# Linear attention with a token mixer: from head pairs to units of 256 tokens, all engines on a planned order

## The chip, the core and the metric

One core of a Trainium2 chip runs the kernel. Its engines are TensorE (PE, with its weight loads shown apart as PEld), VectorE (DVE), ScalarE (ACT), GpSimd (POOL) and SyncE (SP), which here only issues transfers; 16 DMA engines move the data. Each engine takes its instructions strictly in the order in which they were put into its queue, and waits on semaphores for the others. The metric is the device time of one execution in microseconds, the median over the runs.

## The reference, cut to what matters

```python
B, H, S, D = 4, 8, 768, 48
for t in range(S):                                  # float32, per batch and head
    cur   = (u * k[t])[:, None] * v[t][None, :]
    y[t]  = r[t] @ (state + cur)
    state = w[t][:, None] * state + k[t][:, None] * v[t][None, :]
x = y laid out as [B, S, 384]
W = (x @ w_q) @ (x @ w_k).T / 8                     # 64 hidden columns
out = relu(W @ x) @ w_out                           # [B, S, 384] float32
```

Both kernels work in chunks of 128 tokens. With L the running sum of log w inside a chunk, r is scaled by exp(L before t), k by exp(-L at t); the product of the two, masked to earlier tokens, times v gives the part of y that comes from inside the chunk. A state per head pair carries the rest, and u enters as a term on the diagonal. The mixer has no softmax, so W @ x is taken as (x w_q) (T), with T = (x w_k).T @ x summed over all 768 tokens of a batch: the second half of the mixer can start only when a batch's last token has its y.

## The kernel before, in words

For each batch, `prep` runs for four pairs of heads, each over all 768 tokens (6 chunks). It loads w, k, r, v (L127), takes the logarithm (L144), sums it twice on PE (cw), takes two exponentials (L151, L158), multiplies them with r on DVE (`RdS`, L166) and with k on POOL (`KdS`, L168), transposes both on PE (psT) and copies the result out of PSUM (`RKT`, L177). The masked products are `AmB` (L188). POOL also builds the u term in three more passes (L195, L196, L199) with a reduction on DVE between them (L198). Then a loop over the six chunks of the batch carries the state (`SB`, L238), forms `X` (L250) and transposes it (`XT`, L260). After it come the mixer's products, `mixT` (L288), the last product `fps`, its copy `osb` (L296), and one store for each chunk (L297).

The order in each queue is the framework's own: it lets prep of one batch run beside the chunk loop of the one before. All loads and stores go through the SP queue: each load waits for a free one of three buffers of its kind, each store for its osb, and what stands behind waits too. All matmuls go through the helper at L54, so rows of PE are told apart by their tiles.

Of the kernel before, what the change touches and what calls it, by code (L numbers as in the profile page):

```python
# [25 lines left out]
def kernel(  # L26
# [43 lines left out]
    iota1 = consts.tile([C, 1], mybir.dt.int32, tag="iota1")  # L70
    nc.gpsimd.iota(iota1, pattern=[[0, 1]], base=1, channel_multiplier=1)
    bias_px = consts.tile([C, 1], F32, tag="bpx")
    bias_mi = consts.tile([C, 1], F32, tag="bmi")
    bias_c = consts.tile([C, 1], F32, tag="bc")
    nc.scalar.activation(bias_px, iota0, ACT.Copy, bias=0.0, scale=MU)
    nc.scalar.activation(bias_mi, iota1, ACT.Copy, bias=0.0, scale=-MU)
    nc.gpsimd.memset(bias_c, MU * C)

    NB = 3
    LW = []
    RdS = []
    for i in range(NB):
        t = consts.tile([C, NCH, C], BF16, name=f"logw{i}", tag=f"logw{i}")
        nc.gpsimd.memset(t, 0.0)
        LW.append(t)
        t = consts.tile([C, NCH, C], BF16, name=f"RdS{i}", tag=f"RdS{i}")
        nc.gpsimd.memset(t, 0.0)
        RdS.append(t)  # L90
    KdS = []
    PT = []
    for i in range(2):
        t = consts.tile([C, NP, NCH, C], BF16, name=f"KdS{i}", tag=f"KdS{i}")
# [16 lines left out]
    sm = ctx.enter_context(tc.tile_pool(name="sm", bufs=3))
    ps = ctx.enter_context(tc.tile_pool(name="ps", bufs=1, space=bass.MemoryType.PSUM))
    xpool = ctx.enter_context(tc.tile_pool(name="xpool", bufs=2))
    msb = ctx.enter_context(tc.tile_pool(name="msb", bufs=2))
    mout = ctx.enter_context(tc.tile_pool(name="mout", bufs=4))

    def mtile(shape, dtype, name):
        return ps.tile(shape, dtype, name=name, tag="m", bufs=2)

    def prep(b, hp, AmB, RKT, VB, Vd, ptp):  # L120
        n = b * NP + hp
        wG = ld.tile([C, 2 * NCH, D], F32, name="wG", tag="wG")
        kG = ld.tile([C, 2 * NCH, D], F32, name="kG", tag="kG")
        rG = ld.tile([C, 2 * NCH, D], F32, name="rG", tag="rG")
        vG = ld.tile([C, 2 * NCH, D], F32, name="vG", tag="vG")
        for ap, tl in ((w, wG), (k, kG), (r, rG), (v, vG)):
            nc.sync.dma_start(out=tl, in_=ap[b, ds(hp * 2, 2)].rearrange(  # L127
                "h (c p) d -> p (h c) d", p=C))
        if n == 0:
            nc.sync.dma_start(out=u1, in_=u.rearrange("h d -> (h d)"))  # L130
            nc.gpsimd.partition_broadcast(ubc, u1)

        def hcd(t):
            return t.rearrange("p (h c) d -> p h c d", h=2)

        def chd(t):
            return t.rearrange("p (h c) d -> p c h d", h=2)

        def pad(t):
            return t.rearrange("p c (h x) -> p c h x", h=2)[:, :, :, 0:D]  # L140

        logw = LW[n % NB]
        for hh in range(2):
            nc.scalar.activation(logw[:, :, ds(hh * 64, D)],  # L144
                                 wG[:, ds(hh * NCH, NCH)], ACT.Ln,
                                 bias=0.0, scale=LN_SCALE)
        cw1 = ps.tile([C, 2, 512], F32, name="cw1", tag="cw")
        for hh in range(2):
            mm(cw1[:, hh, 0:NCH * D], US128, logw[:, :, ds(hh * 64, D)])
        ecwx = hw.tile([C, 2, NCH, D], BF16, name="ecwx", tag="ecwx")  # L150
        nc.scalar.activation(ecwx.rearrange("p h c d -> p h (c d)"),  # L151
                             cw1[:, :, 0:NCH * D], ACT.Exp,
                             bias=bias_px, scale=1.0)
        cw0 = ps.tile([C, 2, 512], F32, name="cw0", tag="cw")
        for hh in range(2):
            mm(cw0[:, hh, 0:NCH * D], U128, logw[:, :, ds(hh * 64, D)])
        emcw = hw.tile([C, 2, NCH, D], BF16, name="emcw", tag="emcw")
        nc.scalar.activation(emcw.rearrange("p h c d -> p h (c d)"),  # L158
                             cw0[:, :, 0:NCH * D], ACT.Exp,
                             bias=bias_mi, scale=-1.0)  # L160
        for c in range(NCH):
            mm(ptp[:, hp, ds(c, 1)], logw[:, c], ones)

        Rd = RdS[n % NB]
        Kd = KdS[b % 2][:, hp]
        nc.vector.tensor_tensor(pad(Rd), chd(rG),  # L166
                                ecwx.rearrange("p h c d -> p c h d"), ALU.mult)
        nc.gpsimd.tensor_tensor(pad(Kd), chd(kG),  # L168
                                emcw.rearrange("p h c d -> p c h d"), ALU.mult)
        nc.scalar.copy(VB[:, :, ds(hp * 2, 2)], chd(vG))  # L170

        psT = ps.tile([C, 2, 1024], BF16, name="psT", tag="psT")
        for c in range(NCH):
            mm(psT[:, 0, ds(c * C, C)], Rd[:, c], ID128, trans=True)
        for c in range(NCH):
            mm(psT[:, 1, ds(c * C, C)], Kd[:, c], ID128, trans=True)
        nc.vector.tensor_copy(RKT[:, hp], psT[:, :, 0:NCH * C])  # L177

        NG = NCH // 2
        for g in range(2):  # L180
            A = ps.tile([C, 2, 512], F32, name="A", tag="A")
            for cc in range(NG):
                c = g * NG + cc
                for hh in range(2):
                    mm(A[:, hh, ds(cc * C, C)],
                       RKT[ds(hh * 64, D), hp, 1, ds(c * C, C)],
                       RKT[ds(hh * 64, D), hp, 0, ds(c * C, C)])
            nc.vector.tensor_tensor(  # L188
                AmB[:, ds(hp * 2, 2), ds(g * NG, NG)],
                A[:, :, 0:NG * C].rearrange("p h (c t) -> p h c t", c=NG),  # L190
                _rep(_rep(US128, 1, NG), 1, 2), ALU.mult)

        uk = hw.tile([C, 2, NCH, D], F32, name="uk", tag="uk")
        ubs = ubc[:, ds(hp * D2, D2)].rearrange("p (h d) -> p h d", h=2)
        nc.gpsimd.tensor_tensor(uk, hcd(kG), _rep(ubs, 2, NCH), ALU.mult)  # L195
        nc.gpsimd.tensor_tensor(uk, uk, hcd(rG), ALU.mult)  # L196
        diag = hw.tile([C, 2, NCH], F32, name="diag", tag="diag")
        nc.vector.tensor_reduce(diag, uk, axis=AX.X, op=ALU.add)  # L198
        nc.gpsimd.tensor_tensor(Vd[:, :, ds(hp * 2, 2)], VB[:, :, ds(hp * 2, 2)],  # L199
                                _rep(diag.rearrange("p h c -> p c h"), 3, D),  # L200
                                ALU.mult)
# [126 lines left out]
```

## Time and profile before

| | |
|---|---|
| Median of 3 runs (lowest, highest) | 182.39 us (180.18, 184.01) |
| Profiled execution, its span from first to last instruction | 182.1 us |
| Busy: PE, DVE, POOL, ACT | 121.0, 112.7, 95.3, 74.0 us |
| Moved by DMA, mean rate | 24.23 MB, 133 GB/s |
| Mean granted TensorE clock | 0.869 of full speed |

The page gives no other time for the profiled execution than its span; the span lies inside the range of the three runs. No engine is busy for more than two thirds of it, so the page alone names no engine as the limit: what to look for is which wait ends last in each stretch. A matmul's duration on the page is that of one instruction in a pipeline; the time that a row of matmuls takes is read from the starts of successive groups.

### The profile page before, as it was taken

What the parts mean: (1) busy time and instruction counts of PE and PEld (TensorE: products, weight loads), DVE (VectorE), ACT (ScalarE), POOL (GpSimd) and SP (SyncE); (2) the same over time, 40 slices, a digit from 0 to 9 for tenths busy, and PEclk for the clock granted to TensorE, in tenths of its full rate; (3) what the DMA queues carried; (4) which work ended last, traced back from release to release, by engine and by line L of the source; (5) the groups of instructions that cost most, each with busy time, mean ns of one, the idle gap of its engine ahead of it and who ended that gap; (6) DMA issues with size and microseconds to landing.
All of it is one profiled execution on the core that took longest, in us unless ns stands there. A gap on an engine that the chain in (4) does not pass through costs nothing.

```text
span 182.1 us, 3121 instructions
## 1 busy us (share of the span) xinstructions
PE 121.0 (66%) x1200; PEld 74.3 (41%) x1200; DVE 112.7 (62%) x156; ACT 74.0 (41%) x140; POOL 95.3 (52%) x86
## 2 busy tenths in 40 slices
PE   0152178130698787966988986688888964787791
PEld 0121045010465653343765533465564243565240
DVE  6011147469889977644799778179996553744042
ACT  3175473310045446066346461944456232022620
POOL 8410599999728976406993954379586202000000
PEclk9999999999999997585599999657999697557969
DMA  7999999999999300399999908999940240000024
GB/s 127 186 188 187 187 185 158 196 215 157 169 187 168 67 4 2 142 236 200 190 178 191 166 13 237 235 168 200 185 73 0 86 150 27 0 5 0 0 81 178
DMA packets 104000, 24.23 MB, mean 133 GB/s; under 512 B 100529, under 2 KB 103986, under 8 KB 103986
## 3 DMA queue, kind: packets, MB, share of 16 engines
q1 hardware_dynamic: 103186, 23.70, 76.7%
q0 software_dynamic: 800, 0.34, 1.5%
q8 instruction: 9, 0.15, 0.4%
q14 instruction: 5, 0.04, 0.1%
HBM read 19.66 MB, written 4.72 MB: 134 GB/s over the span
## 4 chain that ended last, share of the span: by engine, by line
PE 25%; DVE 23%; issue 18%; POOL 12%; ACT 7%; DMA 7%; SPq 6%; POOLq 1%; ACTq 0%; DVEq 0%
DVE RdS L166 6%; PE psT L54 6%; DVE X L250 5%; SPq L127 5%; DVE RKT L177 5%; POOL uk L196 4%; DMA wG<-in_w_dram 3%; ACT XT L260 3%; POOL uk L195 3%; PE cw L54 3%; POOL Vd L199 3%; PE wq_ps L54 2%; PE fps L54 2%; DVE AmB L188 2%; PE Tps L54 2%
## 5 line engine op out<-in xcount | busy, mean ns | idle before, releaser
L168 POOL TENSOR_TENSOR KdS<-kG,emcw 128x576 bf16<-128x576 f32 x16 | 22.2, 1388 | 41.5 <-ACT emcw L158 33.2
L188 DVE TENSOR_TENSOR AmB<-A,US 128x768 bf16<-128x768 f32 x32 | 30.4, 950 | 5.7 <-PE A L54 4.4
L166 DVE TENSOR_TENSOR RdS<-rG,ecwx 128x576 bf16<-128x576 f32 x16 | 20.8, 1298 | 20.2 <-ACT ecwx L151 14.6
L177 DVE COPY RKT<-psT 128x1536 bf16<-128x1536 bf16 x16 | 15.3, 953 | 19.4 <-PE psT L54 19.3
L195 POOL TENSOR_TENSOR uk<-kG,ubc 128x576 f32<-128x576 f32 x16 | 24.0, 1499 | 0.0
L196 POOL TENSOR_TENSOR uk<-uk,rG 128x576 f32<-128x576 f32 x16 | 23.6, 1476 | 0.6
L199 POOL TENSOR_TENSOR Vd<-VB,diag 128x576 bf16<-128x576 bf16 x16 | 18.7, 1172 | 8.4 <-ACT VB L170 6.2
L54 PE MATMUL A<-RKT 48*128 48x128 bf16 x192 | 17.5, 263 | 7.0 <-DVE RKT L177 4.2
L144 ACT ACTIVATE logw<-wG 128x288 bf16<-128x288 f32 x32 | 12.4, 435 | 23.7 <-PE ptp L54 11.3
L151 ACT ACTIVATE ecwx<-cw,bias_px 128x576 bf16<-128x576 f32 x16 | 11.9, 741 | 24.6 <-PE cw L54 24.5
L54 PEld LDWEIGHTS <-KdS 128*128 128x128 bf16 x176 | 16.1, 123 | 13.7 <-POOL KdS L168 9.9
L54 PEld LDWEIGHTS <-RKT 48*128 48x128 bf16 (+1 forms) x272 | 13.6, 108 | 19.6 <-issue 9.3
L54 PE MATMUL fps<-wout_sb,mixT 128*128 128x384 bf16 x72 | 19.7, 418 | 1.7 <-ACT mixT L288 1.2
L296 DVE COPY osb<-fps 128x384 f32<-128x384 f32 x24 | 13.0, 554 | 12.4 <-PE fps L54 12.2
L54 PE MATMUL cw<-logw,US 128*128 128x288 bf16 x32 | 10.5, 365 | 13.4 <-ACT logw L144 12.9
L260 ACT COPY XT<-xt_ps 128x768 bf16<-128x768 bf16 x12 | 9.6, 799 | 21.4 <-PE xt_ps L54 21.4
L158 ACT ACTIVATE emcw<-cw,bias_mi 128x576 bf16<-128x576 f32 x16 | 11.9, 742 | 11.3 <-PE cw L54 11.2
L54 PE MATMUL psT<-ID,RdS 128*128 128x128 bf16 x96 | 11.4, 272 | 7.5 <-DVE RdS L166 7.5
L54 PE MATMUL cw<-logw,U 128*128 128x288 bf16 x32 | 9.7, 386 | 8.4 <-ACT ecwx L151 8.4
L54 PE MATMUL psT<-ID,KdS 128*128 128x128 bf16 x96 | 12.7, 277 | 2.8 <-POOL KdS L168 2.8
L170 ACT CAST VB<-vG 128x576 bf16<-128x576 f32 x16 | 10.7, 666 | 7.8 <-DMA vG<-in_v_dram 7.7
L54 PE MATMUL Sn<-VB,KdS 128*128 128x96 bf16 x80 | 9.9, 238 | 5.4 <-POOL KdS L168 5.4
(53 smaller groups left out, 181.1 us busy)
## 6 DMA issues: line engine op xcount, KB each, us to landing
wG<-in_w_dram SPq DMA_DIRECT2D x16, 288.0 KB, 5.6
kG<-in_k_dram SPq DMA_DIRECT2D x16, 288.0 KB, 5.3
rG<-in_r_dram SPq DMA_DIRECT2D x16, 288.0 KB, 5.6
vG<-in_v_dram SPq DMA_DIRECT2D x16, 288.0 KB, 5.6
out_dram<-osb SPq DMA_DIRECT2D x24, 192.0 KB, 1.9
wout_sb<-in_moe_w_out_dram POOLq DMA_DIRECT2D x1, 288.0 KB, 4.8
wq_f<-in_moe_w_q_dram SPq DMA_DIRECT2D x1, 96.0 KB, 4.6
wk_sb<-in_moe_w_k_dram POOLq DMA_DIRECT2D x1, 48.0 KB, 4.6
```

Source lines behind the costliest of these rows:

```text
L54: nc.tensor.matmul(o, l, rr, start=start, stop=stop, skip_group_check=sgc, is_transpose=trans)
L144: nc.scalar.activation(logw[:, :, ds(hh * 64, D)], wG[:, ds(hh * NCH, NCH)], ACT.Ln, bias=0.0, scale=LN_SCALE)
L151: nc.scalar.activation(ecwx.rearrange("p h c d -> p h (c d)"), cw1[:, :, 0:NCH * D], ACT.Exp, bias=bias_px, scale=1.0)
L166: nc.vector.tensor_tensor(pad(Rd), chd(rG), ecwx.rearrange("p h c d -> p c h d"), ALU.mult)
L168: nc.gpsimd.tensor_tensor(pad(Kd), chd(kG), emcw.rearrange("p h c d -> p c h d"), ALU.mult)
L177: nc.vector.tensor_copy(RKT[:, hp], psT[:, :, 0:NCH * C])
L188: nc.vector.tensor_tensor(AmB[:, ds(hp * 2, 2), ds(g * NG, NG)], A[:, :, 0:NG * C].rearrange("p h (c t) -> p h c t", c=NG), _rep(_rep(US12 ...
L195: nc.gpsimd.tensor_tensor(uk, hcd(kG), _rep(ubs, 2, NCH), ALU.mult)
L196: nc.gpsimd.tensor_tensor(uk, uk, hcd(rG), ALU.mult)
L199: nc.gpsimd.tensor_tensor(Vd[:, :, ds(hp * 2, 2)], VB[:, :, ds(hp * 2, 2)], _rep(diag.rearrange("p h c -> p c h"), 3, D), ALU.mult)
L260: nc.scalar.copy(XT[:, :, ds((c - 1) * C, 2 * C)], tp)
L296: nc.vector.tensor_copy(osb, fps)
```

## The change

The whole body is new. The unit of work is 256 tokens of one batch over all eight heads (12 units, three for a batch). A load brings one tensor of a unit as 1,024 rows of 384 bytes (two tokens of a head beside each other) instead of 1,536 rows of 192 bytes, into four buffers of its kind; for seven of the twelve units v is loaded in token order instead, by four transfers over 64 partitions each with rows of 192 bytes, 2,048 rows in all; for the other five a PE product with a permutation (vp) sorts it.

The logarithm's sum is formed once and transposed (cw: channels on partitions, tokens on columns, both exponentials from it). r and k are cast to bf16 (c16, mostly on POOL) and transposed raw (rT, kT), the transposed k is copied out (ks), and the exponentials are multiplied in afterwards (RT, KT). The u term is a product on PE (qT, dps, dd) and one POOL pass (Vd). kb and kd turn the scaled k back for the state. The loop of sn, sb, y, x, xt, the mixer's qk, T, mx, rl, fp and the stores follow for each unit, with 256-token tiles. PSUM is one tile of eight banks, PS, from which steps take one or two banks.

Every step is put into a list with an engine, a planned duration and a rank. `Plan.order` gives each engine its steps by rank, walks through them with the planned durations to choose banks and a common order, and the instructions are emitted in that order with the framework's own ordering switched off. ENG gives the engine of each step for the 12 units (A, D, P for ACT, DVE, POOL). PE gets 9 filler products at the start, 26 after the first cw and 16 near the end.

```diff
+def view(t, off, dims, p0=0, pn=128):
+
+    base = t[ds(p0, pn), ds(off, 1)]
+    return dataclasses.replace(base, ap=[list(base.ap[0])] + [list(d) for d in dims])
...
+    def add(self, eng, dur, rank, fn, after=(), fill=None, read=(), lag=100, mode=0,
+            behind=None):
+        s = dict(mode=mode, behind=behind, eng=eng, dur=dur, rank=rank, fn=fn, after=[a for a in after if a is not None],
...
+    def dma(self, issue, dur, rank, fn, after=(), fill=None, read=()):
+
+        i = self.add("SP", issue, rank, fn, after, fill, read, lag=0)
+        m = self.add("DQ", dur, 0, self.nothing, [i], lag=0)
+        return i, self.add(f"L{m['n']}", 1950, 0, self.nothing, [m], lag=0)
...
+        for s in sorted(self.steps, key=lambda s: s["rank"]):
+            if s["eng"] in queues:
+                queues[s["eng"]].append(s)
...
+            if s["eng"] == "SP" and len(moved) >= 3:
+                t = max(t, moved[-3])
...
+            if s["fill"] in ("w", "s"):
+                two = s["fill"] == "w"
+                at = [clear(x) for x in owners]
+                end = 7 if two else 8
...
+            change = e == "PE" and s["mode"] != mode
+            if e == "PE":
+                mode = s["mode"]
+            run(s, t, s["dur"] + self.switch * change)
...
+    PS = ps.tile([C, 4096], F32, name="PS", tag="PS")
+    NB = 4
+    WG = [const([C, HW], F32, f"wg{i}") for i in range(NB)]
...
+    KDS = [const([C, 1024], BF16, f"kd{i}") for i in range(2)]
+    LW = [const([C, 2 * H * 64], BF16, f"lw{i}") for i in range(2)]
...
+    def load_v(b, i, tl):
+
+        for c in range(2):
+            src = v[b, :, ds(i * U + c * C, C)].rearrange("h (q j) d -> j q h d", j=2)
+            for j in range(2):
+                nc.sync.dma_start(out=view(tl, c * DM, [[D, H], [1, D]], p0=64 * j, pn=64),
+                                  in_=src[j])
+
+    def load(b, i, tl, ap):
+        nc.sync.dma_start(
+            out=view(tl, 0, [[D2, H], [1, D2]]),
+            in_=ap[b, :, ds(i * U, U)].rearrange("h (p j) d -> p h (j d)", j=2))
...
+    for _ in range(9):
+        mm(PS[:, ds(0, 512)], Z[:, ds(0, C)], Z)
...
+    ENG = dict(k16="DAPPAPPPPPPP", r16="DPPPPAPPPPPP", KT="DDPDPPPPPPPP", vb="AAAADAAAAAAA",
+               kd="AAADAAAAADAA", xts="ADDADAADAAAD", qks="AAADAAAAAAAA", rl="AAAAAAAAAAAA",
+               os="AAAAAAADDDDD", dd="AAAAAADDAAAD", ks="DDAAADADDAAD")
+    RANK = [14, 0, 0, 0, 0, 15, 0, 0, 0, 1, 0, 0, 2, 0, 0, 5, 0, 0, 0, 0, 1, 1, 3, 1, 5, 2, 5, 10,
...
+    DIRECT = "001011011011"
+    SPLIT = (0, B * NU - 1)
...
+    plan = Plan(kinds, 90)
...
+        for tile_, ap, name in ((wg, w, "wg"), (kg, k, "kg"), (rg, r, "rg"), (vg, v, "vg")):
+            if name == "vg" and direct:
+                issue, land = plan.dma(2600, 2080, STEP * n + OFF["load"],
+                                       lambda tile_=tile_: load_v(b, i, tile_), fill=name)
+            else:
+                issue, land = plan.dma(580, 1440 + 340 * (name == "wg" and n == 0),
+                                       STEP * n + OFF["load"],
...
+            nc.scalar.activation(view(lw, 0, [[64, H], [512, 2], [1, D]]),
+                                 view(wg, 0, [[D2, H], [D, 2], [1, D]]), ACT.Ln,
+                                 bias=0.0, scale=math.exp(-MU))
...
+                op = dict(A=nc.scalar.copy, D=nc.vector.tensor_copy, P=nc.gpsimd.tensor_copy)[e]
+                op(view(dst, 0, [[64, H], [512, 2], [1, D]]),
+                   view(src, 0, [[D2, H], [D, 2], [1, D]]))
...
+            t["cw"] = cw = wtile("cw")
+            for hp in range(NP):
+                for j in range(2):
+                    for c in range(2):
+                        mm(cw[:, ds(c * 512 + hp * C, C)],
+                           lw[ds(c * 64, 64), ds(j * 512 + hp * 128, 128)],
...
+                nc.scalar.activation(sb("en", [C, 1024])[:, cols(cs, 512)],
+                                     t["cw"][:, cols(cs, 512)], ACT.Exp, bias=0.0, scale=-1.0)
...
+                nc.scalar.activation(
+                    view(ep, cs[0] * NP * EW + 66, [[EW, NP * len(cs)], [-65, 2], [1, 64]]),
...
+                t[name] = x = stile(BF16, name)
+                for hp in range(NP):
+                    for j in range(2):
+                        mm(view(x, hp * C + j * 64, [[512, 2], [1, 64]]),
+                           src[:, ds(j * 512 + hp * 128, 128)], ID16, trans=True)
...
+            copy(kse, sb("ks", [C, 1024]), t["kT"])
...
+            nc.vector.tensor_tensor(sb("qT", [C, 1024]), t["rT"], t["ks"], ALU.mult)
...
+                nc.vector.tensor_tensor(
+                    view(sb("RT", [C, 1024]), cs[0] * 512, [[C, n4], [64, 2], [1, 64]]),
+                    view(t["rT"], cs[0] * 512, [[C, n4], [64, 2], [1, 64]]),
...
+                e = nc.vector if kte == "D" else nc.gpsimd
+                e.tensor_tensor(sb("KT", [C, 1024])[:, cols(cs, 512)], t["ks"][:, cols(cs, 512)],
+                                t["en"][:, cols(cs, 512)], ALU.mult)
...
+                nc.gpsimd.tensor_copy(sb("VB", [C, 2 * DM]), vg)
...
+                nc.gpsimd.tensor_copy(view(sb("v16", [C, 2 * DM]), 0, [[D, H], [DM, 2], [1, D]]),
+                                      view(vg, 0, [[D2, H], [D, 2], [1, D]]))
...
+                        mm(x[:, ds(c * 512, DM)], PM[ds(c * 64, 64), ds(j * C, C)],
+                           t["v16"][ds(c * 64, 64), ds(j * DM, DM)], start=(j == 0), stop=(j == 1))
...
+                copy(vbe, view(sb("VB", [C, 2 * DM]), 0, [[DM, 2], [1, DM]]),
+                     view(t["vp"], 0, [[512, 2], [1, DM]]))
...
+                    mm(x[:, ds(c * H + hp * 2, 2)], t["qT"][:, ds((c * NP + hp) * C, C)],
+                       UB[:, ds(hp * 2, 2)], start=(c == 0 and hp == 0), stop=True)
...
+                nc.gpsimd.tensor_tensor(
+                    sb("Vd", [C, 2 * DM])[:, cols(cs, DM)], t["VB"][:, cols(cs, DM)],
...
+                        mm(x[:, ds(hh * 512 + hp * C, C)],
+                           t["KT"][ds(hh * 64, D), ds((c * NP + hp) * C, C)],
+                           t["RT"][ds(hh * 64, D), ds((c * NP + hp) * C, C)])
...
+                nc.vector.tensor_tensor(
+                    view(sb(f"AM{c}", [C, 1024]), 0, [[C, 8], [1, C]]),
+                    view(t[f"A{c}"], 0, [[C, 8], [1, C]]),
...
+                    mm(t["kb"][:, ds(cp * C, C)], t["KT"][:, ds(cp * C, C)], ID16, trans=True)
...
+                copy(kde, view(KDS[n % 2], cs[0] * 512, of), view(t["kb"], cs[0] * 512, of), gv)
...
+                    if old is not None:
+                        mm(x[:, ds(0, DM)], ID16, old.tile, start=True, stop=False)
+                    for hp in range(NP):
+                        mm(x[:, ds(hp * D2, D2)], KDS[n % 2][:, ds((c * NP + hp) * C, C)],
+                           t["VB"][:, ds(c * DM + hp * D2, D2)],
...
+                    nc.vector.tensor_tensor(view(x, 0, [[D, H], [1, D]]),
+                                            view(t[f"sn{c}"], 0, [[D, H], [1, D]]),
+                                            view(t["ptm"], c * 8, [[1, 8], [0, D]]), ALU.mult)
...
+                    mm(y[:, ds(c * 512 + h * D, D)],
+                       t[f"AM{c}"][:, ds(hh * 512 + hp * C, C)],
+                       t["VB"][:, ds(c * DM + h * D, D)], start=(h == 0), stop=(old is None))
+                if old is not None:
+                    for hp in range(NP):
+                        mm(y[:, ds(c * 512 + hp * D2, D2)], t["RT"][:, ds((c * NP + hp) * C, C)],
...
+                nc.vector.scalar_tensor_tensor(
+                    view(X["t"], (2 * i + c0) * DM, [[DM, ncs], [1, DM]]),
+                    view(t["y"], c0 * 512, [[512, ncs], [1, DM]]), gx,
+                    view(t["Vd"], c0 * DM, [[DM, ncs], [1, DM]]), ALU.mult, ALU.add)
...
+                    mm(x[:, ds(wqo, nq)], wq_sb[:, ds(kt * C, C)], XT[:, ds(kt * nq, nq)],
+                       start=(end and kt == 0), stop=(kt == NK - 1))
...
+                    mm(x[:, ds(dt * U, U)], batch["TS"][:, ds(dt * 128, 128)],
+                       view(batch["QK"], ii * 384 + C, [[64, 2], [C, 2], [1, 64]]),
+                       start=(dt != 1))
...
+                    relu(e, view(t[f"MX{ii}"], cs[0] * C, [[U, NK], [1, w_]]),
+                         view(t[f"mx{ii}"], cs[0] * C, [[U, NK], [1, w_]]))
...
+                            mm(x[:, ds(c * 512, DM)],
+                               t[f"MX{ii}"][:, ds(kt * U + c * C, C)],
+                               wo_sb[:, ds(kt * DM, DM)], start=(kt == 0), stop=(kt == NK - 1))
...
+                if end and ii == NU - 1 and p == 0:
+                    add("A", 550, "st", f_st(nc.scalar), more=6 * ii, cs=cs, use=[go], lag=2000)
+                else:
+                    issue, land = plan.dma(
+                        500, 580 * len(cs), STEP * n + OFF["st"] + 6 * ii, f_st(nc.sync),
+                        [go.by[c] for c in cs])
...
+    for n in range(B * NU):
...
+        if n == 0:
+            warm(26, 215, [state["cw"]])
...
+    for s, at in zip(plan.steps, RANK):
+        s["rank"] = at
+    with tc.manual_schedule():
+        for s in plan.order():
+            now["step"] = s
+            s["fn"]()
```

## Rows read from the trace of the kernel before

**Rows 1.** The page's busy time, share of span and instructions of each engine.

```profile
PE 121.0 (66%) x1200; PEld 74.3 (41%) x1200; DVE 112.7 (62%) x156; ACT 74.0 (41%) x140; POOL 95.3 (52%) x86
```

**Rows 2.** Windows by stretch: engines' busy us (instructions), then PEclk, DMA share, GB/s.

```profile
4.50:9.00 4.50, 0.87 (x8) 0.49 (x8) 0.00 (x0) 0.73 (x2) 2.12 (x4) 1.00 1.41 186
82.00:100.00 18.00, 14.76 (x188) 10.29 (x186) 14.39 (x22) 9.51 (x17) 12.91 (x10) 0.74 1.16 190
100.00:112.00 12.00, 10.21 (x79) 5.12 (x76) 9.52 (x14) 5.29 (x11) 9.23 (x7) 1.00 0.64 128
114.00:115.00 1.00, 0.39 (x7) 0.30 (x7) 0.00 (x0) 0.96 (x3) 0.00 (x0) 1.00 0.98 296
152.00:170.00 18.00, 13.73 (x149) 9.76 (x149) 9.20 (x15) 3.34 (x5) 0.70 (x1) 0.62 0.00 1
```

**Rows 3.** The SP queue's waits: waiter, releaser, total us, times, longest.

```profile
SPq L297 <- DVE osb L296: 66.4, 19, 25.7
```

**Rows 4.** Timeline of the SP queue: start, us, transfer issued.

```profile
60.27 0.37 SPq L127 DMA_DIRECT2D rG<-in_r_dram  x1
73.10 3.65 SPq L297 DMA_DIRECT2D out_dram<-osb  x4
```

**Rows 5.** Timeline of ACT at the start.

```profile
4.46 0.78 ACT L144 ACTIVATE logw<-wG 128x288 bf16<-128x288 f32 x2 [1.96 <-DMA wG<-in_w_dram]
```

**Rows 6.** Groups by form on ACT: shapes, count, then busy us, mean ns.

```profile
L260 ACT COPY XT<-xt_ps 128x768 bf16<-128x768 bf16 x12 | 9.6, 799 | 21.4 <-PE xt_ps L54 21.4
...
L288 ACT ACTIVATE mixT<-mps 128x384 bf16<-128x384 f32 x24 | 10.8, 489 | 1.9 <-PE mps L54 1.7
```

**Rows 7.** The same on DVE.

```profile
L188 DVE TENSOR_TENSOR AmB<-A,US 128x768 bf16<-128x768 f32 x32 | 30.4, 950 | 5.7 <-PE A L54 4.4 <-PE mps L54 1.0
...
L177 DVE COPY RKT<-psT 128x1536 bf16<-128x1536 bf16 x16 | 15.3, 953 | 19.4 <-PE psT L54 19.3
L296 DVE COPY osb<-fps 128x384 f32<-128x384 f32 x24 | 13.0, 554 | 12.4 <-PE fps L54 12.2 <-DMA out_dram<-osb 0.2
```

**Rows 8.** The same on POOL.

```profile
L199 POOL TENSOR_TENSOR Vd<-VB,diag 128x576 bf16<-128x576 bf16 x16 | 18.7, 1172 | 8.4 <-ACT VB L170 6.2 <-DVE diag L198 2.2
...
L86 POOL MEMSET logw<- 128x768 bf16 x3 | 2.2, 738 | 0.0
```

**Rows 9.** Timelines of DVE and POOL: the same multiplication at two times.

```profile
10.55 0.76 DVE L166 TENSOR_TENSOR RdS<-rG,ecwx 128x576 bf16<-128x576 f32 x1 [6.37 <-ACT ecwx L151]
...
38.77 6.48 DVE L166 TENSOR_TENSOR RdS<-rG,ecwx 128x576 bf16<-128x576 f32 x1
43.25 1.39 POOL L195 TENSOR_TENSOR uk<-kG,ubc 128x576 f32<-128x576 f32 x1
44.71 1.80 POOL L196 TENSOR_TENSOR uk<-uk,rG 128x576 f32<-128x576 f32 x1
```

**Rows 10.** Timeline of PE at the lower, then the higher clock.

```profile
87.51 0.85 PE L54 MATMUL psT<-ID,RdS 128*128 128x128 bf16 x6
88.15 0.85 PE L54 MATMUL psT<-ID,KdS 128*128 128x128 bf16 x6
...
93.07 0.36 PE L54 MATMUL Y<-VB,AmB 128*128 128x48 bf16 x8
93.27 0.33 PE L54 MATMUL Y<-SB,RKT 128*128 128x96 bf16 x4
93.44 0.33 PE L54 MATMUL Sn<-SB,ID 128*128 128x384 bf16 x1
93.60 0.33 PE L54 MATMUL Sn<-VB,KdS 128*128 128x96 bf16 x4
...
94.33 0.51 PE L54 MATMUL psT<-ID,RdS 128*128 128x128 bf16 x6 [0.23 <-DVE RdS L166]
94.67 0.28 PE L54 MATMUL psT<-ID,KdS 128*128 128x128 bf16 x2
```

**Rows 11.** The page's transfers: KB each, us from issue to landing.

```profile
out_dram<-osb SPq DMA_DIRECT2D x24, 192.0 KB, 1.9
```

More of the change, by code (lines that the diff above doesn't have):

```diff
@@ L1 @@
 import dataclasses
+import heapq
 import math
@@ L41 @@
     C = 128
+    U = 2 * C
+    NU = S // U
     NCH = S // C
@@ L70 @@
[L70 to L94, printed above, removed]
-        nc.vector.memset(t, 0.0)
-        KdS.append(t)
-        t = consts.tile([C, NCH, H], F32, name=f"pt{i}", tag=f"pt{i}")
-        nc.vector.memset(t, 0.0)
-        PT.append(t)
@@ L111 @@
[L111 to L128, printed above, removed]
-        if n == 0:
[L130 to L201, printed above, removed]
@@ new lines, with wtile, stile @@
+    for name in ("lw", "r16", "k16", "ep"):
+        kinds[name] = 2
+    for name in ("en", "ks", "qT", "RT", "KT", "ptm", "v16", "VB", "dd", "Vd", "AM0", "AM1", "KD", "XT"):
+        kinds[name] = NS
+    kinds["MX"] = 4
+    plan = Plan(kinds, 90)
+    now = {}
+    def wtile(name):
+        return PS[:, ds(now["step"]["buf"]["bank"][0] * 512, 1024)]
+    def stile(dtype, name):
+        x = PS[:, ds(now["step"]["buf"]["bank"][0] * 512, 512)]
+        return x if dtype == F32 else x.bitcast(dtype)
@@ new lines, in took, with copy @@
+    def took(eng, cols, half=False, by=False):
+        if eng == "A":
+            return (265 if by else 164) + int(cols * 0.83)
+        if eng == "P":
+            return 140 + int(cols * 1.94)
+        return (210 if by else 150) + int(cols * (0.52 if half else 1.04))
+    def copy(eng, o, i, by=None):
+        if eng == "A":
+            if by is None:
+                nc.scalar.copy(o, i)
+            else:
+                nc.scalar.activation(o, i, ACT.Copy, bias=0.0, scale=by)
+        elif by is None:
+            nc.vector.tensor_copy(o, i)
+        else:
+            nc.vector.tensor_scalar_mul(o, i, by)
@@ new lines, in relu, with warm, f, __init__ @@
+    def relu(eng, o, i):
+        if eng == "A":
+            nc.scalar.activation(o, i, ACT.Relu)
+        else:
+            nc.vector.tensor_scalar_max(o, i, 0.0)
+    def warm(count, dur, after=()):
+        def f():
+            mm(stile(F32, "warm"), Z[:, ds(0, C)], Z)
+        for _ in range(count):
+            s_ = plan.add("PE", dur, 1 << 20, f, after, fill="s", lag=0)
+            plan.reads(s_, s_, True)
+        return s_
+    class Got:
+        def __init__(self):
+            self.by = {}
+            self.first = None
+        def put(self, step, cs):
+            self.first = self.first or step
+            for c in cs:
+                self.by[c] = step
```

609 lines of the change are left out of this document (494 added, 115 removed), and 34 rows, old and new, of the table RANK.

## Prediction, before the changed kernel had run

> **What bounds the kernel now.** I read the busy shares first: PE leads with 121.0 of 182.1 us, DVE has 112.7, POOL 95.3, ACT 74.0 [rows 1]. With no engine above 66%, waits set the end, so I went to the windows and the SP queue. Early on, only loads run and move 186 GB/s; at 82 to 100 us the loads still run at 190 GB/s while PE is busy 14.76 of 18 us, at a granted clock of 0.74 [rows 2]. In between there are holes: the SP queue waits 66.4 us in total for the copies that feed stores, once for 25.7 us [rows 3], and the queue shows what stands behind it: after a load issued at 60.27 nothing is issued until the stores at 73.10 [rows 4]. The last stretch has no loads at all: from 152 to 170 us DMA moves 1 GB/s, POOL is idle (0.70 us), DVE is half idle, and PE runs at 0.62 of its clock [rows 2]. So the kernel is a load-limited prep, stalls at each batch's change, and a tail of some 30 us of one batch alone. None of this is an engine at its limit, and a change that lowers the work of every queue and fills the holes can pay twice.
>
> **DMA.** Now 98,304 load rows of 192 bytes; 186 GB/s is 1.03 ns a row over all 16 engines [rows 2]. The new loads are 41 of 1,024 rows of 384 bytes (393 KB), and for seven units 2,048 rows of 192 bytes. The trace has no 384-byte row. At the least it costs what a 192-byte row costs: 41 x 1,024 x 1.03 = 43 us; at the most, the same bytes per second: 16.1 MB / 186 = 87 us. The second of 296 GB/s, in which loads are mixed with stores of longer rows [rows 2], shows that the engines can move more than 186; I take that: 54 us. Add 7 x 2,048 x 1.03 = 15 us, stores 4.72 MB at 296 = 16 us, weights 2 us: 87 us, between 76 and 120. SP issues 41 loads, 28 pieces of v, 3 weights and 14 stores, 86 in all, at 0.37 us when the queue is free [rows 4]: 32 us, hidden. The weights leave POOL's queue for SP's, and u goes to ACT's; one issue each, behind the first loads. The new wait is that a store still stands ahead of later loads on SP; with four buffers of 256 tokens for each tensor the loads run up to four units ahead, so some 30 us of cover lie behind it.
>
> **ACT.** 799 ns for 768 columns and 489 for 384 [rows 6] give 0.81 ns a column and 179 ns fixed. Logarithm 12 x 0.80 = 9.6; exponentials 20 x 1.01 + 8 x 0.59 = 24.8; 36 copies and relus of 768 columns, 28.8; 27 of 384, 13.2; ks 6 x 1.01 = 6.0; small ones 2.2. Sum 85 us, more than today's 74: ACT takes over PSUM copies.
>
> **DVE.** 950 ns for 768 and 554 for 384 columns give 1.03 a column and 158 fixed; the bf16 copy of 1,536 columns from PSUM in 953 gives 0.52 a column [rows 7]. Masked products am 24 x 1.21 = 29.1; sb 20 x 0.55 = 11.1; x 11.6; thirty operations of 1,024 bf16 columns at 0.69 (qT, RT, KT, ks) 20.6; halves of these 2.5; the remaining copies 11.7. Sum 87 us. Not shown is whether a multiplication of bf16 with one input in PSUM (qT, RT) runs at the copy's 0.52: at 1.03 it costs 13 us more. I take 0.52, the nearest row in place and type, and keep both. The setup (some 5 us of memsets) lies under the first load.
>
> Today one multiplication with two SBUF inputs took 0.76 us at 10.55 and 6.48 us at 38.77; the second ended only after POOL's instructions, which stand nearly end to end, left a gap at 44.64 [rows 9]. The new DVE steps read PSUM in one input, so this loss goes, except for the four KT of units 0, 1 and 3, which have two SBUF inputs. Each can cost nothing or 5.7 us more; early units have a less filled POOL, so I take 1 us each and keep 23 us for the range. The Trainium skill ("SBUF — State Buffer", section "Who interferes with whom") says that a DVE instruction with two SBUF inputs and a GpSimd instruction that reads SBUF shut each other out for whole instructions; rows 9 agree, and by that rule these four are the places where the change can still lose.
>
> **POOL.** The bf16 product takes 1,172 ns for 576 columns, 2.03 a column [rows 8]. KT 8 x 2.08 + 2 x 1.04 = 18.7; Vd 12 x 1.56 = 18.7; 31 casts of k, r and v, 768 columns each, not shown: between a memset of that size, 0.74, and the two-input price, 1.56. A cast reads one stream, so I take 1.0: 31 us. Small ones and setup 6. Sum 74, between 66 and 92; today 95.3.
>
> **PE.** From starts at the higher of its two clocks (2.4 GHz): six transposes in 0.34 us (57 ns each), eight 48-column products in 0.20, four of 96 in 0.17, one of 384 in 0.16 [rows 10]. A unit: cw and A 32 products that use half the rows, 0.6 to 0.9 us each set, 1.2 taken; rT and kT 0.91; kb 0.38; vp 0.18 (mean); dps 0.20; sn 0.50; y 0.68; xt 0.34; qk 0.51; T 0.32; mx 0.33; fp 0.96. Sum 6.5 us, 78 for 12. At the lower clock (1.2 GHz), where the same twelve transposes start every 107 ns [rows 10], it is 157. The fillers cost 5 to 10 us of PE while it would wait.
>
> **The sum.** ACT 85, DVE 87 + 4, DMA 87, PE 78 at full clock, POOL 74: no engine has a long lead, so the steady part lasts for DVE's work divided by how well the fixed order packs it. The best-packed engine today is PE, 14.76 of 18 us (0.82) and 10.21 of 12 (0.85) [rows 2]; I take 0.87, a little above, as each engine now has work of several units to hand. The head: the first load is used at 4.46 us today [rows 5]; with 393 instead of 295 KB some 5. The tail after the last x: xt, xts, qk, its copy, the last T, its copy, mx, relu, fp, copy, each 0.3 to 0.6 us, near 5, then a store that lands in 1.9 [rows 11], and the other two units' outputs beside it: 9. About 4 of DVE's 91 us lie in that tail: 5 + 87 / 0.87 + 9 = 114; if ACT (85, of which 6 lie in the tail) set the pace, 5 + 79 / 0.87 + 9 = 105. The KT term and ACT's lead are the soft ends; I forecast 111. The profiled span, 182.1, is within 0.3 of the median, 182.39, so nothing is added.
>
> **Rivals.**
> PE's clock. Before, PE got 0.74 and 0.62 in stretches in which it was 82 and 76% busy [rows 2]. With 78 us of work in a shorter span it may get the same: 78 / 0.74 = 105, 78 / 0.62 = 126 us of PE, divided by 0.87 and with head and tail 135 to 159. Against it: 26 fillers and a shorter span per product; the stretch from 100 to 112 us is at 1.00 [rows 2]. Chance 0.11.
> DMA by bytes. If 384-byte rows move no faster than 186 GB/s, DMA needs 120 us, and the last unit's 12 to 15 follow: 134. For it: no row shows such a transfer. Against: 296 GB/s. The Trainium skill ("DMA: Bandwidth & Descriptors", section "Specifications") asks for 512 bytes or more for line rate; the new rows stay under that, and by that rule this case is the nearer one, though the rule gives no price for 384. Chance 0.07.
> The order isn't kept or doesn't hold: each queue runs in order, and where planned durations are off, one late step (a POOL cast at 1.56, say) holds everything behind it. Packing then falls to today's best share over the span, 0.66 [rows 1]: 5 + 87 / 0.66 + 9 = 146. Chance 0.04.
> Slower: PSUM is one tile, PS. If accesses to it are kept apart by the tile and not by its banks, every fill by PE and every copy out of it by ACT or DVE follow one another: 78 + 74 (ACT without logarithms and casts) + 83 (DVE without KT and casts) = 235 us before any handover. It decides as soon as the separation is by tile; then nothing else matters. The rows of before cannot exclude it, because its PSUM tiles are separate. Chance 0.04.
>
> **Chances.** The forecast has 0.74, its own range 100 to 128: the low end is DVE at 83 us packed at 0.97, the high end qT and RT at the slower rate. Of the rivals the DMA case and the near end of the clock case fit below 136. So the range is 100 to 136 and leaves out about 0.2. A change within 2% cannot be told from none here. Faster 0.95, slower 0.04, the rest between.
>
> **What would show it.** Right: ACT and DVE busy over 75% of a span near 110, loads without holes, PEclk mostly 1.0, each load of 393 KB about 1.3 us of DMA time, casts on POOL near 1.0 us, qT and RT near 0.69. Wrong: POOL casts above 1.3 us, long KT on DVE, PEclk near 0.7 in the middle, DMA share full to the end, or each bank's fill waiting for another bank's copy.

## The result, and the profile after

The changed kernel takes 108.17 us (median of four runs, 107.16 to 109.91), the kernel before 183.2 us beside it (also four runs). Some executions of either kernel are one to four per cent slower than its others without a change in the work, so the ratio, 0.591 (95% interval 0.585 to 0.598), and all times and differences below are taken from the faster ones: 107.31 us for the changed kernel (107.16 and 107.46), and 74 us gained. The forecast was 111 us, range 100 to 136. The profiled execution took 107.46 us, and its span is 105.2 us: 2.3 us lie outside the span. The prediction added nothing for that, since the page of before gave the span alone.

The page's busy times, which answer to [rows 1], then its lines for slices of a fortieth of the span (2.63 us each): the granted clock has no line because it is full throughout.

```profile
PE 96.2 (91%) x1506; PEld 70.2 (67%) x1506; DVE 88.1 (84%) x138; ACT 79.9 (76%) x123; POOL 71.0 (67%) x92
...
DMA  1999999999999898989997969998997870033564
GB/s 28 298 324 325 325 323 270 238 297 175 312 316 264 148 272 230 288 172 310 325 311 142 213 123 269 350 289 209 288 255 143 303 307 18 0 153 150 199 243 160
```

Where PE led at 66% before, four engines are now between 67 and 91%, and DMA has work without a hole up to the 33rd slice. The same windows by stretch as in [rows 2], here of the changed kernel (busy us and count of PE, PEld, DVE, ACT, POOL; then PEclk, DMA share, GB/s):

```profile
4.40:92.42 88.02, 81.91 (x1426) 62.94 (x1424) 79.36 (x114) 74.16 (x112) 67.83 (x74) 1.00 0.94 247
5.00:10.00 5.00, 4.17 (x47) 2.47 (x48) 4.32 (x13) 3.74 (x9) 0.19 (x1) 1.00 1.17 323
4.40:70.54 66.14, 60.03 (x1044) 45.33 (x1041) 60.03 (x88) 56.19 (x83) 51.47 (x57) 1.00 1.03 266
60.00:70.00 10.00, 8.38 (x147) 6.20 (x143) 8.17 (x10) 7.90 (x13) 7.14 (x9) 1.00 0.99 260
80.00:90.00 10.00, 10.00 (x186) 7.92 (x185) 8.88 (x13) 8.06 (x16) 8.54 (x10) 1.00 0.54 184
90.00:105.00 15.00, 13.50 (x117) 8.13 (x115) 7.41 (x15) 6.65 (x14) 0.00 (x0) 1.00 0.42 158
```

From 5 to 10 us only rows of 384 bytes move: 323 GB/s, where rows of 192 bytes gave 186 [rows 2], so one load of 393 KB takes 1.22 us. The clock column holds 1.00 in every stretch, against 0.74 and 0.62 before. From the first use of a load (4.40) to 70.54 the DMA share is 1.03, so DMA is full, and PE and DVE are busy for 91% each. Between 60 and 70 us all engines are less full than around it, with DMA as full as ever. From 80 to 90 us DMA is half idle and PE has no idle time.

The prices, which answer to [rows 6 to 8] (groups by form: count, busy us, mean ns):

```profile
L619 DVE TENSOR_TENSOR AM<-PS,US 128x1024 bf16<-128x1024 f32 x24 | 28.9, 1220 | 1.1 <-PE PS L181 0.7
...
L498 ACT ACTIVATE en<-PS 128x1024 bf16<-128x1024 f32 x10 | 10.1, 1026 | 0.2 <-PE PS L181 0.2
...
L475 POOL CAST r<-rg 128x768 bf16<-128x768 f32 x10 | 8.7, 870 | 1.6 <-DMA rg<-in_r_dram 1.5
...
L529 DVE TENSOR_TENSOR qT<-PS,ks 128x1024 bf16<-128x1024 bf16 x12 | 8.2, 683 | 0.4 <-PE PS L181 0.4
...
L536 DVE TENSOR_TENSOR RT<-PS,ep 128x1024 bf16<-128x1024 bf16 x10 | 6.9, 686 | 0.5 <-PE PS L181 0.2
...
L547 DVE TENSOR_TENSOR KT<-ks,en 128x1024 bf16<-128x1024 bf16 x2 | 1.5, 770 | 0.1
```

The longest waits of the changed kernel (waiter, releaser, total us, times, longest us), without those of PE's weight loads:

```profile
ACT lw L467 <- DMA wg<-in_w_dram: 5.1, 4, 2.3
POOL v L566 <- DMA vg<-in_v_dram: 4.5, 2, 4.3
DVE X L707 <- PE PS L181: 2.8, 7, 0.6
```

The two longest are waits for loads, but 2.3 of the 5.1 us and 4.3 of the 4.5 us are the first load of w and of v, at the start; after that each wait is short. The chain of waits (start us, us, what) shows what holds the later part:

```profile
63.30 6.31 DMA kg<-in_k_dram
...
69.66 0.84 POOL k L475
...
70.54 22.65 PE PS L181 x390
```

A load issued at 63.30 holds the chain for 6.3 us, and then 390 products on PE follow one another without a wait for 22.65 us: the loads that still come in that time do not hold PE up. The last x, behind which the prediction's tail begins, ends at 92.42:

```profile
91.28 1.14 DVE L707 SCALAR_TENSOR_TENSOR X<-PS,gx,Vd 128x384 bf16<-128x384 f32 x2 [0.57 <-PE PS L181]
```

### The profile page after: what moved, and what is told of

Read it like the earlier page. It is cut to its first block, busy times and chain, and to the rows that moved or that the text cites. A ratio compares the mean times of both kernels' runs of the same rounds, so it can differ in the third digit from the quotient of the medians.

```text
span 105.2 us, 3714 instructions
## 1 busy us (share of the span) xinstructions
PE 96.2 (91%) x1506; PEld 70.2 (67%) x1506; DVE 88.1 (84%) x138; ACT 79.9 (76%) x123; POOL 71.0 (67%) x92
## 4 chain that ended last, share of the span: by engine, by line
PE 51%; DVE 14%; DMA 13%; issue 7%; POOL 5%; ACT 4%; SPq 4%; DVEq 0%; ACTq 0%; POOLq 0%
PE PS L181 51%; DMA wg<-in_w_dram 7%; DMA kg<-in_k_dram 6%; SPq L226 3%; DVE SB L666 2%; DVE RT L536 2%; POOL KT L547 2%; DVE qT L529 2%; DVE KT L547 2%; POOL Vd L601 1%; ACT MX L381 1%; SPq L230 1%; ACT kd L373 1%; DVE X L707 1%; DVE kd L265 1%
## 5 line engine op out<-in xcount | busy, mean ns | idle before, releaser
L619 DVE TENSOR_TENSOR AM<-PS,US 128x1024 bf16<-128x1024 f32 x24 | 28.9, 1220 | 1.1 <-PE PS L181 0.7
L547 POOL TENSOR_TENSOR KT<-ks,en 128x1024 bf16<-128x1024 bf16 (+1 forms) x10 | 19.3, 1934 | 1.2 <-ACT en L498 0.6
L601 POOL TENSOR_TENSOR Vd<-VB,dd 128x768 bf16<-128x768 bf16 (+1 forms) x14 | 18.4, 1318 | 2.2 <-ACT dd L371 1.3
L181 PE MATMUL PS<-Z 128*128 128x512 bf16 x51 | 16.2, 424 | 1.5 <-DVE uT L248 1.2
L707 DVE SCALAR_TENSOR_TENSOR X<-PS,gx,Vd 128x768 bf16<-128x768 f32 (+1 forms) x13 | 12.3, 955 | 3.3 <-PE PS L181 2.8
L181 PEld LDWEIGHTS <-KT 48*128 48x128 bf16 (+1 forms) x272 | 10.7, 95 | 6.3 <-issue 3.8
L181 PE MATMUL PS<-wo,MX 128*128 128x384 bf16 x72 | 13.5, 326 | 0.1
L504 ACT ACTIVATE ep<-PS 128x1024 bf16<-128x1024 f32 (+1 forms) x14 | 12.7, 922 | 0.9 <-PE PS L181 0.9
L498 ACT ACTIVATE en<-PS 128x1024 bf16<-128x1024 f32 (+1 forms) x14 | 12.5, 904 | 0.5 <-issue 0.3
L666 DVE TENSOR_TENSOR SB<-PS,ptm 128x384 bf16<-128x384 f32 x20 | 11.1, 553 | 1.5 <-PE PS L181 1.3
L181 PE MATMUL PS<-RT,KT 48*128 48x128 bf16 x192 | 9.2, 217 | 1.4 <-POOL KT L547 0.5
L181 PE MATMUL PS<-ID,k 128*128 128x128 bf16 x96 | 7.4, 220 | 2.2 <-POOL k L475 1.4
L181 PEld LDWEIGHTS <-MX 128*128 128x128 bf16 x72 | 6.7, 98 | 3.9 <-issue 0.3
L181 PEld LDWEIGHTS <-Z 128*128 128x128 bf16 x51 | 5.0, 105 | 6.0 <-issue 2.3
L181 PE MATMUL PS<-CM,lw 64*128 64x128 bf16 x192 | 7.8, 223 | 1.1 <-ACT XT L371 0.7
```

Of the source, the lines that this page charges most:

```text
L181: nc.tensor.matmul(o, l, rr, start=start, stop=stop, skip_group_check=True, is_transpose=trans)
L498: nc.scalar.activation(sb("en", [C, 1024])[:, cols(cs, 512)], t["cw"][:, cols(cs, 512)], ACT.Exp, bias=0.0, scale=-1.0)
L504: nc.scalar.activation(view(ep, cs[0] * NP * EW + 66, [[EW, NP * len(cs)], [-65, 2], [1, 64]]), t["cw"][:, cols(cs, 512)], ACT.Exp, bias=0 ...
L547: e.tensor_tensor(sb("KT", [C, 1024])[:, cols(cs, 512)], t["ks"][:, cols(cs, 512)], t["en"][:, cols(cs, 512)], ALU.mult)
L601: nc.gpsimd.tensor_tensor(sb("Vd", [C, 2 * DM])[:, cols(cs, DM)], t["VB"][:, cols(cs, DM)], view(t["dd"], cs[0] * H, [[1, len(cs) * H], [0 ...
L619: nc.vector.tensor_tensor(view(sb(f"AM{c}", [C, 1024]), 0, [[C, 8], [1, C]]), view(t[f"A{c}"], 0, [[C, 8], [1, C]]), view(US, 0, [[0, 8], ...
```

## The experiments

**What does a microsecond more on each engine cost?** Five kernels add about a microsecond of work per unit to one resource each, with unchanged output; the plan and its order stay as they are (edits shortened).

```diff
# e_dve, behind am of the first chunk        # e_act, behind the logarithm
+ nc.vector.tensor_tensor(XG[768 columns],   + nc.scalar.copy(XB, XA)
+     A0[768 columns], US, ALU.mult)
# e_pool, behind the cast of v               # e_pe, ahead of cw
+ nc.gpsimd.tensor_copy(XB[960], XA[960])    + for _ in range(5): mm(cw[512], Z, Z)
# e_dma, behind the load of w
+ load(b, i, XG, ap)
```

> One more masked product of 768 columns on VectorE in each of the 12 units, written to a spare tile: about 0.95 us each, 11.4 us of DVE. If DVE sets the pace, as the prediction had it, the time rises by 10 to 11.4 us. If the loads or PE set it, by 0 to 4 us. If all engines are about equally close to the path, by 5 to 9 us.

> One more copy of 1,024 columns on ScalarE in each of the 12 units, behind the logarithm: about 1.0 us each, 12 us of ACT. If DVE sets the pace: 2 to 6 us more, since ACT has 8 us less work than DVE. If the loads or PE set it: 0 to 4. If all are equally close: 5 to 9.

> Five more products of 512 columns with zeros on TensorE at the start of each unit's cw: 12 x 5 x 0.215 = 12.9 us of PE at full clock. If PE sets the pace (half of the chain of the changed kernel is PE), 11 to 13 us more. If DVE or the loads set it, 0 to 4. If all are equally close, 5 to 9.

> The load of w is issued twice in each of the 12 units, the second time into a spare tile that nothing reads: 12 x 1.2 us = 14.6 us of DMA and 12 issues on SP. If the loads set the pace, which end near 82 us, 12 to 14.6 us more. If DVE or PE sets it, 0 to 5. If all are equally close, 6 to 10.

> One more copy of 960 bf16 columns on GpSimd in each of the 12 units, behind the cast of v: about 1.0 us each, 12 us of POOL, which is busy for 71 of 105 us. If only DVE, PE or the loads set the pace: 0 to 3 us more. If the order is so tight that a late step on any engine holds the rest: 5 to 9.

Measured, against 107.31 (the added work from the rows of these runs, for PE from the busy times, for DMA from the expectation):

| | work added, us | time, us | more, us |
|---|---|---|---|
| e_dma | 14.6 | 123.46 (123.12, 123.80) | 16.2 |
| e_pe | 13.0 | 115.03 (114.94 to 115.53) | 7.7 |
| e_dve | 11.4 | 111.62 (111.20 to 112.06) | 4.3 |
| e_pool | 12.0 | 109.28 (108.02 to 109.42) | 2.0 |
| e_act | 12.5 | 108.37 (108.07 to 109.12) | 1.1 |

Loads come through in full and more, PE by over half, DVE by over a third. POOL's and ACT's differences are about as large as the spread between runs of one kernel (1.4 us), so they are told apart neither from each other nor clearly from nothing. DVE as the pace asked for 10 us or more and is ruled out. What fits best is "the loads set the pace", but not alone: PE's 7.7 lies in the band of "all equally close". DVE's 4.3 is not DVE's time alone, since the added product also holds a bank of PSUM: in that run PE waits 6.0 us in all for it (`PE PS L181 <- DVE XG L628: 6.0, 9, 1.4`).

The pages' shares of the chain that ended last, in the order changed kernel, e_dma, e_pe, show the lead pass between two resources:

```profile
PE 51%; DVE 14%; DMA 13%; issue 7%; POOL 5%; ACT 4%; SPq 4%; DVEq 0%; ACTq 0%; POOLq 0%
DMA 33%; PE 25%; SPq 22%; issue 7%; POOL 6%; ACT 3%; DVE 2%; POOLq 0%
PE 87%; DVE 4%; POOL 3%; ACT 2%; issue 2%; DVEq 0%; ACTq 0%; POOLq 0%
```

Why DMA costs more than it adds was not settled; two windows of that run show one candidate (columns as above):

```profile
20.00:40.00 20.00, 15.25 (x237) 12.15 (x237) 11.33 (x15) 11.97 (x18) 13.09 (x13) 0.83 1.01 253
60.00:80.00 20.00, 11.99 (x199) 9.95 (x197) 10.98 (x15) 11.10 (x15) 11.78 (x13) 0.75 0.91 223
```

PE is busy for 76 and 60% and its clock is granted at 0.83 and 0.75, so its products take longer too (PE is busy for 101.4 us in all, against 96.2). How much of the 1.6 us beyond the added work is the clock's was not measured apart.

**Less work for DMA.**

```diff
-    lambda tile_=tile_: load_v(b, i, tile_), fill=name)
+    lambda tile_=tile_: load(b, i, tile_, v), fill=name)
```

> v of the seven units by one plain load of 384-byte rows instead of four transfers of 192-byte rows, so the tokens of v stand in the wrong order in these units; all else is the same work. DMA has 7 x (2.1 - 1.2) = 6 us less, SP 21 issues less. If the loads set the pace: 4 to 6 us faster. If DVE or PE sets it: 0 to 1.5.

103.74 us (103.27 to 104.61): 3.6 us less, just short of what the loads' theory asked and well beyond the other's 1.5. (The kernel leaves out the sorting of v in these units; it prices the transfers only.) In this run the last load is issued at 69.50 us (first fence), in the changed kernel its last four from 77.22 on (second):

```profile
69.50 0.37 SPq L230 DMA_DIRECT2D vg<-in_v_dram  x1
```

```profile
77.22 2.66 SPq L226 DMA_DIRECT2D vg<-in_v_dram  x4
```

The loads end some 8 to 10 us earlier. Divided by the seven groups, with 1.2 for the plain load counted back in, that is an estimate of 2.4 us or more for four transfers over 64 partitions, above the 2.1 forecast. Only 3.6 of these microseconds reach the end, because what follows is PE's: its stretch without a wait begins earlier and is longer than the 22.65 us of the changed kernel, and PE has 72% of the chain instead of 51%:

```profile
63.65 26.20 PE PS L181 x458
```

**Longer rows, undone.**

```diff
-        nc.sync.dma_start(
-            out=view(tl, 0, [[D2, H], [1, D2]]),
-            in_=ap[b, :, ds(i * U, U)].rearrange("h (p j) d -> p h (j d)", j=2))
+        src = ap[b, :, ds(i * U, U)].rearrange("h (p j) d -> j p h d", j=2)
+        for j in range(2):
+            nc.sync.dma_start(out=view(tl, j * D, [[D2, H], [1, D]]), in_=src[j])
```

> Each plain load is issued as two transfers of 1,024 rows of 192 bytes, one for each token of a pair, instead of one of 1,024 rows of 384 bytes: the same bytes in the same places. At 1.03 ns a row 41 loads take 2.1 us instead of 1.2, 37 us of DMA more, and SP issues 41 more. If the loads set the pace: 30 to 45 us more, 138 to 153. If DMA only seems full and the rest sets the pace: below 120.

132.71 us (131.38 to 132.79): 25.4 us more, less than the 30 to 45 expected and far above 120. Its page:

```profile
GB/s 77 221 217 218 218 178 221 219 169 251 186 190 194 218 138 206 216 184 142 221 182 150 229 177 145 183 208 205 228 202 167 232 124 363 128 0 123 164 246 195
DMA packets 103857, 24.62 MB, mean 188 GB/s; under 512 B 101536, under 2 KB 102688, under 8 KB 103840
```

These transfers of 1,024 short rows ran at 217 to 221 GB/s, not at the 186 of before, so a load costs 1.8 us instead of 2.1: 41 x (1.8 - 1.22) = 24 us, nearly the whole difference. So the longer rows are worth a third of the 74 us once everything else is in place. The run also issues 41 transfers more on SP, and does not tell row length and number of transfers apart.

**The order.** Two kernels keep every instruction of the engines and change who orders them (edits shortened).

```diff
# e_sched: the planned order is only handed over
-    with tc.manual_schedule():
-        for s in plan.order(): ...
+    for s in plan.order(): ...
# e_listrank: unit after unit, as the steps are written down
-    for s, at in zip(plan.steps, RANK): s["rank"] = at
+    for at, s in enumerate(plan.steps): s["rank"] = at
```

> The steps are handed over in the same planned order, but the framework may order each queue itself again, as for the kernel before. If its order is about as good as the planned one, 107 to 115 us. If not, 120 to 150, with the waits of the SP queue and idle time between units back.

> The steps keep their engines, tiles and transfers, but each engine takes them in the order in which the units are written down, one unit after the other, instead of by the ranks. If the gain comes from fewer and cheaper operations and longer rows alone, the time stays below 125 us. If the planned order is a large part of it, each unit's chain of products, copies and exponentials is exposed in part: 140 to 180 us, with PE busy for 50 to 65% of the span and a lower granted clock.

With the framework's order 153.76 us (153.20, 154.31), 0.850 of before (0.842 to 0.857): just beyond the worse of the two cases. In list order 279.25 us (278.45 to 279.66), half as long again as before and far beyond its range. Their busy times, first of the framework's order (a span of 154.7 us), then of the list order (276.7 us):

```profile
PE 120.7 (78%) x1506; PEld 83.6 (54%) x1506; DVE 88.6 (57%) x138; ACT 80.9 (52%) x123; POOL 70.7 (46%) x92
```

```profile
PE 160.9 (58%) x1506; PEld 104.1 (38%) x1506; DVE 90.8 (33%) x138; ACT 83.6 (30%) x123; POOL 70.0 (25%) x92
```

The work of DVE, ACT and POOL is that of the changed kernel to within 5%; only PE's grows, with its clock (0.879 and 0.605 of full speed over these runs). What differs is waiting, and with the framework's order it is the engines that wait for one another:

```profile
POOL ptm L553 <- ACT ep L504: 22.2, 7, 5.3
POOL KT L547 <- ACT en L498: 19.7, 4, 6.6
```

The second of these is 0.6 us in the changed kernel. The SP queue does stand 34.5 us at one store, but behind its last load. So of the 74 us gained, some 27 come with the new operations and rows in the framework's hands, and 46 more with the planned order; going unit after unit gives all of it back and 98 us besides. The planned order was not tried on the old operations, so these two parts, like the third above, hold for this sequence of changes only.

**The fillers** (edit shortened).

```diff
-    for _ in range(9): mm(PS[:, ds(0, 512)], Z[:, ds(0, C)], Z)
-            mm(stile(F32, "warm"), Z[:, ds(0, C)], Z)
+            pass
```

> The 51 filler products on PE are left out, about 11 us of PE at full clock. If they only fill PE's waiting time and do not matter for its clock, the time stays within 1 us. If they keep the clock up, the granted clock falls in the first 20 us and near the end and the time rises by 3 to 8 us. If they stand in PE's way, it falls by 2 to 5.

106.36 us (105.82 to 106.92), 0.9 us less, a ratio to before of 0.589 (0.582 to 0.596) that overlaps the changed kernel's 0.591: no clear difference, as in the first case, and no gain from the fillers. The clock falls in one stretch (0.91), and hardly near the end (0.98 from 90 to 105 us):

```profile
20.00:40.00 20.00, 17.99 (x324) 14.53 (x319) 17.12 (x24) 17.06 (x26) 16.02 (x17) 0.91 1.04 259
```

In the changed kernel fifteen of the fillers stand behind the last useful product, and run to 104.1 of 105.2 us:

```profile
100.67 3.40 PE L181 MATMUL PS<-Z 128*128 128x512 bf16 x15
```

**A better version, tried.** The runs above point to fewer v transfers and no fillers; the edit makes `DIRECT` all zeros, gives ACT the seven new copies, puts the 21 new steps at ranks beside those of the units that had them, and drops the fillers.

> All twelve units load v by one plain load of 384-byte rows and sort it on PE, as five did, with the new steps put at hand-chosen places in the planned order, and the 51 filler products are left out. DMA has 6 us less or more, 21 SP issues less; PE gets 7 x 0.33 = 2.3 us more and 11 us of fillers less; ACT gets 7 x 0.8 = 5.6 us more. If the loads set the pace and ACT has slack: about 4 us off for DMA, 1.2 back for PE, 0.3 back for ACT and 1.8 off for the fillers, so near 103.5 us against 108. If the new steps' places are bad or ACT has no slack: 107 to 115.

115.87 us (115.49 to 116.43), 8.6 us slower than the changed kernel. Its chain shows one reason:

```profile
20.13 5.99 DMA vg<-in_v_dram
...
26.24 0.82 POOL v L530
27.06 1.44 POOL Vd L565
28.50 2.08 POOL KT L511
...
30.63 6.68 PE PS L181 x104
```

The casts of v stand a few places further ahead in POOL's queue than before the edit. Here POOL is idle for 5.32 us ahead of such a cast, until its load has landed; Vd and KT stand behind it. PE waits 3.75 us for the cast and 2.72 for KT, DVE 5.08 for Vd. DMA is not what lacks: it has nearly nothing to do from 80 to 90 us (2 GB/s). Where the rest of the 8.6 us went was not traced, and whether the same idea with better places gains is open.

**The stalls of before.**

```diff
-            nc.sync.dma_start(out=out[b, ds(c * C, C), :], in_=osb)
+            nc.scalar.dma_start(out=out[b, ds(c * C, C), :], in_=osb)
```

> The kernel before, with its 24 stores issued from ACT's queue instead of SP's, so that no load stands behind a store. If the stalls of the loads behind stores cost the kernel before 7 to 13 us at each of three changes of batch, as its SP queue suggests, it gets 15 to 30 us faster. If the loads have no free buffer then anyway, or ACT's waits take the place of SP's, it changes by less than 5 us.

181.29 us (180.15 to 182.65), ratio 1.004 (0.995 to 1.013): nothing. Three timelines of this run at the first change of batch show why (SP, POOL, ACT; start us, us, and in brackets the idle time before and its releaser):

```profile
62.00 1.32 SPq L127 DMA_DIRECT2D wG<-in_w_dram  x1
75.79 0.37 SPq L127 DMA_DIRECT2D kG<-in_k_dram  x1
...
72.84 1.40 POOL L195 TENSOR_TENSOR uk<-kG,ubc 128x576 f32<-128x576 f32 x1
74.31 1.40 POOL L196 TENSOR_TENSOR uk<-uk,rG 128x576 f32<-128x576 f32 x1
...
73.82 5.02 ACTq L297 DMA_DIRECT2D out_dram<-osb  x6
78.94 1.11 ACT L144 ACTIVATE logw<-wG 128x288 bf16<-128x288 f32 x3 [6.54 <-DMA out_dram<-osb]
```

With no store in it, the SP queue has nearly the same hole: kG is issued at 75.79, when POOL has just used up an older pair of k and r at 75.71, where the kernel before issued its stores at 73.10 and a load at 76.84. The buffers were not free either. Meanwhile ACT, whose w had been loaded, waits 6.54 us behind its own stores. So both of the expected ways to nothing are seen, and the run does not tell what the stores alone cost before. ACT's logarithm comes at the same time in both kernels, 78.81 before and 78.94 here.

## Why the prediction was right, and where it was not

The number held, and partly by luck. **The step that failed is the sum**: it let DVE set the pace at a packing of 0.87, between 105 us with ACT and 114 with DVE in the lead, and took 111. DVE's 11.4 us more cost 4.3 at most; the loads' 14.6 us cost 16.2. In its place the runs show a pace that the loads and PE share: DMA is full until 70.5 us, when PE has waited for the load of kg issued at 63.30 and its cast; then PE works for 22.65 us without a wait, and the tail follows.

In the prediction's own terms, 111 is a head of 5, a steady part of 97 up to the last x, and a tail of 9. Measured are 4.4, then 88.0 (to 92.42), 12.8 to the end of the span, and 2.3 outside it, in all 107.5. The steady part was 9 us too long, the tail 3.8 too short and the outside was not counted, so these errors partly cancelled. In the steady part PE is busy for 81.9 us (0.93) and DVE for 79.4 (0.90), so a packing near 0.87 was a good guess, for an engine that was not the pace.

**Terms that held.** qT and RT ran at 683 and 686 ns, the lower of the two ends, as taken. DVE was busy 88 us, 82 without its 6 us of setup, against 87; ACT 80 against 85; POOL 71 against 74, its casts 0.82 to 0.87 us against 1.0. A plain load took 1.22 us against 1.3, the four-piece load of v more than the 2.1 forecast (2.4 or more, the estimate above). With these prices, and stores and weights as forecast, DMA's sum is an estimate of 50 + 17 + 16 + 2 = 85 us, near the 87 forecast. It was the sum closest to DVE's, and was passed over as something that hides under it.

**PE's term.** Forecast were 78 us, the least but POOL's 74. Without fillers PE was busy for 88.1 us (the run above), and 390 products in 22.65 us, at some 121 products a unit, make 7.0 us a unit against the 6.5 forecast, or 85 us for twelve. The fillers' 8 us lie in the forecast 5 to 10. With 85 to 88 us PE stands beside DMA's 87, and so it is PE that takes over where the loads let go.

**KT on DVE.** The term of 1 us each was too dear. The two whole ones took 0.77 us; one of the halves took 1.05 us beside 0.43 for the other (start us, us):

```profile
9.24 0.43 DVE L547 TENSOR_TENSOR KT<-ks,en 128x512 bf16<-128x512 bf16 x1
...
10.64 0.82 POOL L566 CAST v<-vg 128x768 bf16<-128x768 f32 x1 [4.31 <-DMA vg<-in_v_dram]
10.69 1.05 DVE L547 TENSOR_TENSOR KT<-ks,en 128x512 bf16<-128x512 bf16 x1
```

At 10.64 POOL begins a cast of 0.82 us, so one of the four met, by all appearance, what [rows 9] showed, at a cost of 0.6 us instead of the 4 us taken for all four.

**The reading of before.** "Stalls at each batch's change" were laid on stores ahead of loads. With the stores elsewhere the hole stays, as the loads have no free buffer; the stores' own share stays open, since ACT then waited in SP's place. That the changed kernel filled these holes stands; that stores made them does not.

**The rivals.** PE's clock: granted at 1.00 throughout; without fillers 0.983 over the run. DMA by bytes: 323 GB/s instead of 186. The order does not hold: it held. Lost to the framework's order it costs 153.8 us, near the rival's 146, and unit after unit far more. PS kept apart as a whole: PE was busy for all of the 10 us from 80 to 90 while DVE and ACT, which mostly read PS, were busy 8.88 and 8.06, so fills and copies overlap, and 107 us leave no room for the rival's 235.

## What to carry to other kernels

When several engines and DMA are forecast within ten per cent of each other, say that the pace is open, and settle it with a microsecond of extra work on each in turn: the busiest engine by the page (PE, 91%) and the fullest by the sum (DVE) were not the ones that answered most. Look at what else the added work holds, as the DVE product held a bank of PSUM. A queue's longest wait names what stands at its head; only moving that away shows whether the work behind could have started. And a planned order can be worth more than half of a gain (46 of 74 us here, with the new operations in place), but it is fitted to them: with 21 new steps at hand-chosen places the kernel lost 8.6 us.

## What was not expected of the hardware

Rows of 192 bytes moved at 186 GB/s in transfers of 1,536 rows and at 217 to 221 in transfers of 1,024. The two also differ in which rows lie beside each other, and no run tells what makes the difference. Rows of 384 bytes moved at 323, so a row of twice the length took 1.22 us / 1,024 = 1.19 ns over all engines against 1.03 before. The clock fell under added loads (0.75 in a stretch with PE 60% busy) in a kernel whose clock was otherwise full, also without fillers but for one stretch (0.91, with PE 90% busy).
